# Where VectorE's folds and its small routing steps stand among the top-k scans, in an attention and experts kernel

## The chip, the cores and the metric

The kernel runs on one core of a Trainium2 chip. The metric is the time of one execution on the device, in microseconds, and the figure given for a kernel is the median of several executions. The core has five engines that work at the same time and wait for each other by semaphores: TensorE (matrix products and transposes; PE in the profile, and PEld for its weight loads), VectorE (DVE), ScalarE (ACT), GpSimd (POOL) and SyncE (SP), which issues most of the transfers. Each engine takes its instructions in the order in which they stand in its queue.

## The reference, cut to what matters

Attention keeps, for each query, the keys whose score is among the 32 largest, and its result, rearranged to 4608 rows of 512, goes through a layer of eight experts in which each row is sent to one expert.

```python
# B, H, S, D = 8, 8, 576, 64
scores = scale * np.matmul(q, k.transpose(0, 1, 3, 2))
kth = np.partition(scores, -top_k, axis=-1)[..., -top_k:-top_k + 1]    # top_k = 32
scores = np.where(scores >= kth, scores, -1000000000.0)
attn = np.exp(scores - np.max(scores, axis=-1, keepdims=True))
attn = attn / (np.sum(attn, axis=-1, keepdims=True) + 1e-09)
x = np.matmul(attn, v)                       # then to (B*S, H*D) = (4608, 512)

logits = x @ w_gate                          # 8 experts
expert_idx = np.argmax(logits, axis=1)
probs = np.exp(logits - logits.max(-1, keepdims=True))
probs /= probs.sum(-1, keepdims=True) + 1e-09
gate_w = probs[np.arange(N), expert_idx]
# rows sorted by expert, for each expert e:
h = np.maximum(x_sorted[lo:hi] @ w1[e], 0.0)     # 512 -> 1024
y_sorted[lo:hi] = h @ w2[e]                      # 1024 -> 512
out = gate_w[:, None] * y                        # back in the old order
```

## The kernel before, in words

**Units, groups and iterations.** A unit is two heads of one batch: 8 batches by 4 units. The 576 queries of each head are four tiles of 128 and a rest of 64; the rests of the two heads share one tile. So a unit has nine score tiles of 128 by 576, which are worked on in five groups: four pairs (the same tile of both heads; groups 0 to 3) and a single tile (group 4). One iteration of the main loop (L756) does one group, so there are 160 iterations, 20 for a batch. The order of instructions on TensorE, ScalarE and VectorE is the order of this text (`manual_schedule`, L818); on GpSimd most steps are held to it by `in_turn`.

**One iteration i.** VectorE searches the threshold of group i (`search`, L254). First, `fold` (L246) takes the larger and the smaller of columns k and k + 288 of the scores, so that the scans go over 288 columns and not 576. Then four rounds of `max` (the eight largest, L273) and `match_replace` (strike them out, L282) give the 32 largest of the larger halves, one `max` (L278) the eight largest of the smaller halves, and two small steps (L291 and L295) the threshold `thr`. GpSimd makes `low` of it (L297) and `over` (L300), a sign of whether the search was sure. ScalarE makes of scores and `low` a large number below the threshold and 0 above (Relu, L309), GpSimd subtracts it from the scores (`less`, L318), ScalarE takes the exponential and its row sums `z` (L329), and in the next iteration TensorE transposes the weights (L343, L352) and ScalarE copies them out of PSUM (L346, L355). In the same iteration ScalarE copies the scores of group i + 3 from PSUM (L243), behind the Relu, and TensorE multiplies those of group i + 4 (L234).

**Folds.** The folds of group i + 1 stand in the search of group i, before its last round (`between`, L761). A pair's search folds the next pair; where a single tile follows, it folds that and the pair behind it, and the single tile's search folds nothing.

**Ends of units.** `ending` (L665) is a generator that goes on at named places of the loop (`at_place`, L721): value products (L373), the transposes of the result (L379), `divisors` (L394: `doubt`, the sums with an epsilon, their reciprocals and a copy from the upper half of the partitions to the lower), `logits` and `rows` (L402, L412: GpSimd scales by the reciprocals). Behind the last unit of a batch come `route` (L418) and `table` (L493).

**Routing.** `route` finds each row's expert (`oh` is one where the row's expert is), takes the exponential of the logits, and on TensorE counts the rows before each one with the same expert (L436) and the rows of each tile of 128 (L437). ScalarE copies both to SBUF (`rk`, L440). VectorE sums the tiles' counts up to `base` and to the new `run` (L445), adds them to the ranks, picks the row's own (`posi`), and the divisor of the gate (L459 to L461). Then GpSimd scatters the batch's rows to DRAM (`x_rows`, L466) by five indirect DMAs, one an iteration. `table` works on one partition: which blocks of 128 rows have become full, as a list of expert and place for the next blocks.

**Expert blocks.** A block is 128 rows of one expert, in 16 pieces of TensorE's work. From the third batch on, pieces are spread over the iterations as far as blocks are full: 4, 4, 5, 4, 5 and 4 of them are announced by the tables of batches 1 to 6, and a batch's rate begins at its iteration `FIRST`. In the last batch, from iteration `ARRIVED` on, all but the pieces of two blocks are spread over what is left; those two cover the last routing. The other 14 of 40 blocks come behind the loop. `load_block` (L540) reads the table on SyncE and loads rows and weights, two blocks ahead.

**PSUM.** `bank` (L199) gives one of two banks in turn, for transposes, value products and the rank product alike.

Of the kernel before, what the change touches and what calls it, by code (L numbers as in the profile page):

```python
# [18 lines left out]
TOP_K = 32  # L19
# [24 lines left out]
def kernel(  # L44
# [94 lines left out]
    e_less = iota_f("e_less", [P, E], [[1, E]], base=-E)  # L139
    e_at = iota_f("e_at", [P, E], [[CAP, E]])  # L140
# [18 lines left out]
    doubt = const.tile([P, NT], F32, name="doubt")  # L159
# [7 lines left out]
    nc.vector.memset(done, 0.0)  # L167
# [45 lines left out]
    def open_unit(n):  # L213
        n.z = k.small.tile([P, NT], F32, name="z")
        n.over = None if k.exact else k.small.tile([P, NT], F32, name="over")
# [30 lines left out]
    def fold(tiles, s):  # L246

        m2 = slice(0, len(tiles))
        hl = k.att.tile([P, 2, 2, HF], F32, name="hl") if len(tiles) == 2 else k.att.tile([P, 2, 1, HF], F32, name="hl1", bufs=1)
        nc.vector.tensor_tensor(hl[:, 0, m2, :], s[:, m2, 0, :], s[:, m2, 1, :], op=ALU.max)  # L250
        nc.vector.tensor_tensor(hl[:, 1, m2, :], s[:, m2, 0, :], s[:, m2, 1, :], op=ALU.min)
        return hl

    def search(n, tiles, s, hl, begun, between):  # L254
# [5 lines left out]
        if k.exact:  # L260
            src = [s[:, m, :, :].rearrange("p j k -> p (j k)") for m in m_all]
            width = S
        else:
            src = [hl[:, 0, m, :] for m in m_all]
            width = HF
        scr = k.att.tile([P, 2, width], F32, name="scr")
        nbias = k.small.tile([P, 2], F32, name="nbias", bufs=3)
        R = TOP_K // 8
        for r in range(R):
            if r == R - 1:  # L270
                between()
            for m in m_all:
                nc.vector.max(out=tops[:, m, r * 8:(r + 1) * 8], in_=src[m])  # L273
            if r == 0:
                in_turn(nc.gpsimd.tensor_scalar_mul(nbias[:, m2], tops[:, m2, 0], -scale))
                if not k.exact:
                    for m in m_all:
                        nc.vector.max(out=tops[:, m, TOP_K + 1:TOP_K + 9], in_=hl[:, 1, m, :])  # L278
                begun()
            if r < R - 1:  # L280
                for m in m_all:
# [3 lines left out]
                    )  # L285
                    src[m] = scr[:, m, :]
# [107 lines left out]
    def divisors(n):  # L394
        rz = rz_of[n.u % 2]
        if not k.exact:
            nc.vector.tensor_tensor(doubt, doubt, n.over, op=ALU.max)
        nc.vector.tensor_scalar_add(rz[:, 0:NT], n.z, EPS)
        nc.vector.reciprocal(rz[:, 0:NT], rz[:, 0:NT])
        nc.vector.tensor_copy(rz[0:ST, NT:NT + 1], rz[ST:P, NT - 1:NT])  # L400

# [16 lines left out]
    def route(x, lg):  # L418

        mx = k.small.tile([P, KC], F32, name="mx")  # L420
        nc.vector.tensor_reduce(mx, lg, axis=AX.X, op=ALU.max)
        oh = k.small.tile([P, KC, E], F32, name="oh")
        nc.vector.tensor_tensor(oh, lg, _inner(mx[:, :], E), op=ALU.is_ge)
        nc.vector.tensor_tensor(oh, oh, _ins(e_less[:, :], 1, KC), op=ALU.mult)
        idx = k.small.tile([P, KC], F32, name="idx")
        nc.vector.tensor_reduce(idx, oh, axis=AX.X, op=ALU.min)
        nc.vector.tensor_tensor(oh, _ins(e_less[:, :], 1, KC), _inner(idx[:, :], E), op=ALU.is_equal)
        nc.vector.memset(oh[ST:P, NC, :], 0.0)

        nc.vector.tensor_tensor(lg, lg, _inner(mx[:, :], E), op=ALU.subtract)  # L430
        yield
        nc.scalar.activation(lg, lg, AF.Exp)
        yield
        rp = bank("rank")
        ohf = oh[:, :, :].rearrange("p t e -> p (t e)")
        nc.tensor.matmul(rp[:, 0:KC * E], before, ohf, start=True, stop=True)  # L436
        nc.tensor.matmul(rp[:, 256:256 + KC * E], ones, ohf, start=True, stop=True)  # L437
        yield
        rk = k.small.tile([P, 2, KC * E], F32, name="rk")
        nc.scalar.copy(rk, rp[:, :].rearrange("p (a w) -> p a w", a=2)[:, :, 0:KC * E])  # L440
        yield
# [492 lines left out]
```

## Time and profile before

| | us |
|---|---|
| median of 7 executions | 1630.79 (1627.06 to 1636.61) |
| the profiled execution | 1630.93 |
| its span, first to last instruction | 1628.9 |
| batches 0 to 7: time from one batch's last threshold to the next one's (the first from 10.4) | 150.3, 160.1, 164.7, 168.5, 170.1, 172.4, 168.3, 170.3 |
| last threshold of the loop | 1335.4 |
| VectorE, top-8 scans (L273, L278), 1440 instructions | 592.3 busy |
| VectorE, strike-outs (L282), 864, with their loads of values | 447.0 busy |
| VectorE, folds (L250, L251), 320 | 253.3 busy |
| GpSimd, `less` (L318), 288 | 404.4 busy, 1423 ns each |

The table's busy times are sums of the recorded durations. Records of one engine can overlap: a scan is recorded with 0.45 us, but the next one starts 0.36 us after it. So what an instruction costs its engine is better read from the distance between starts in the timeline. A group's line also names the idle time of the engine before it and what ended it; only on the engine that is full does that time count. TensorE's granted clock differs between the parts: 0.78 between 40 and 160 us, where there are no expert blocks, and 0.93 to 0.95 in batches 3 to 7.

### The profile page before, as it was taken

What the parts mean: (1) busy time and instruction counts of PE and PEld (TensorE: products, weight loads), DVE (VectorE), ACT (ScalarE), POOL (GpSimd) and SP (SyncE); (2) the same over time, 40 slices, a digit from 0 to 9 for tenths busy, and PEclk for the clock granted to TensorE, in tenths of its full rate; (3) what the DMA queues carried; (4) which work ended last, traced back from release to release, by engine and by line L of the source; (5) the groups of instructions that cost most, each with busy time, mean ns of one, the idle gap of its engine ahead of it and who ended that gap; (6) DMA issues with size and microseconds to landing.
All of it is one profiled execution on the core that took longest, in us unless ns stands there. A gap on an engine that the chain in (4) does not pass through costs nothing. (4 is left out here: it accounts for less than half of the span.)

```text
span 1628.9 us, 25051 instructions
## 1 busy us (share of the span) xinstructions
PE 1334.3 (82%) x7874; PEld 868.6 (53%) x7874; DVE 1284.2 (79%) x4261; ACT 917.1 (56%) x1937; POOL 667.1 (41%) x993
## 2 busy tenths in 40 slices
PE   5666766664889889978987998799898998799996
PEld 3333433332555555545654655555565656566764
DVE  7999999999999999999998999999989972000000
ACT  4666656665676576657666766667666762111111
POOL 3444454445445454435444544455455442000000
PEclk8777677777899899989998999899998999899998
DMA  1000010001624244344446433334353545788783
GB/s 60 24 23 23 23 49 26 24 24 49 245 90 146 99 150 141 136 147 149 140 177 230 156 140 139 124 135 167 139 174 140 198 154 190 268 322 292 288 332 129
DMA packets 102192, 230.69 MB, mean 142 GB/s; under 512 B 5150, under 2 KB 25630, under 8 KB 102048
## 3 DMA queue, kind: packets, MB, share of 16 engines
q1 hardware_dynamic: 95904, 210.06, 36.3%
q0 software_dynamic: 6144, 18.92, 3.2%
q8 instruction: 65, 1.06, 0.3%
q14 instruction: 79, 0.65, 0.1%
HBM read 207.68 MB, written 22.33 MB: 141 GB/s over the span
## 5 line engine op out<-in xcount | busy, mean ns | idle before, releaser
L318 POOL TENSOR_TENSOR w<-s,w 128x576 f32<-128x576 f32 x288 | 404.4, 1423 | 287.1 <-ACT w L309 287.1
L273 DVE MAX8 tops<-scr 128x8 f32<-128x288 f32 x864 | 356.8, 451 | 3.3
L575 PEld LDWEIGHTS ph<-xTs,w 128*128 128x128 f32 x2560 | 300.7, 193 | 31.7 <-issue 29.0
L575 PE MATMUL ph<-xTs,w 128*128 128x128 f32 x2560 | 312.2, 278 | 5.7 <-DMA w<-in_moe_w_dram 3.1
L309 ACT ACTIVATE w<-s,low 128x576 f32<-128x576 f32 x288 | 208.9, 769 | 190.3 <-POOL low L297 188.4
L584 PE MATMUL py<-w,hT 128*128 128x512 f32 x640 | 308.5, 614 | 6.3 <-ACT hT L580 6.3
L234 PE MATMUL sc<-qkb 64*128 64x288 f32 (+1 forms) x1280 | 243.9, 506 | 70.2 <-ACT s L243 63.6
L282 DVE MATCH_REPLACE8 scr<-tops,scr 128x288 f32<-128x288 f32 x576 | 251.9, 446 | 0.0
L329 ACT ACTIVATE w<-w,nbias 128x576 f32<-128x576 f32 x288 | 221.6, 772 | 1.8 <-POOL w L318 1.8
L343 PE MATMUL wTm<-ident,w 128*128 128x128 f32 x1152 | 180.1, 295 | 42.9 <-ACT oT L375 33.7
L234 PEld LDWEIGHTS sc<-qkb 64*128 64x128 f32 (+1 forms) x1280 | 123.9, 207 | 143.6 <-ACT s L243 80.7
L343 PEld LDWEIGHTS wTm<-ident,w 128*128 128x128 f32 x1152 | 138.7, 150 | 110.2 <-ACT oT L375 41.0
L297 POOL TENSOR_SCALAR low<-thr 128x2 f32<-128x2 f32 (+1 forms) x160 | 35.0, 219 | 361.3 <-DVE thr L295 342.6
L584 PEld LDWEIGHTS py<-w,hT 128*128 128x128 f32 x640 | 114.2, 194 | 117.5 <-issue 106.1
L243 ACT COPY s<-sc 128x576 f32<-128x576 f32 x288 | 170.1, 638 | 9.9 <-PE sc L234 9.9
L373 PE MATMUL po<-wT,vb 128*64 128x288 f32 x1024 | 172.6, 490 | 0.6 <-ACT wT L348 0.6
L352 PE MATMUL wTl<-ident,w 128*64 128x128 f32 x288 | 65.4, 304 | 125.2 <-ACT wT L346 123.8
L346 ACT COPY wT<-wTm 128x512 f32<-128x512 f32 x256 | 140.1, 606 | 11.2 <-PE wTm L343 11.1
L250 DVE TENSOR_TENSOR hl<-s 128x576 f32<-128x576 f32 (+1 forms) x160 | 129.3, 808 | 12.4 <-ACT s L243 12.4
L590 POOL DMA_INDIRECT out_dram<-y,xg x40 | 41.9, 1048 | 236.1 <-ACT y L587 232.3
L373 PEld LDWEIGHTS po<-wT,vb 128*64 128x64 f32 x1024 | 81.3, 165 | 89.1 <-issue 35.0
L282 DVE MATCH_REPLACE8 scr<-tops,hl 128x288 f32<-128x288 f32 x288 | 125.7, 444 | 0.0
(123 smaller groups left out, 1362.8 us busy)
## 6 DMA issues: line engine op xcount, KB each, us to landing
w<-in_moe_w_dram SPq DMA_DIRECT2D x80, 2048.0 KB, 9.1
qkb<-in_qk_dram SPq DMA_DIRECT2D x32, 576.0 KB, 5.0
xg<-x_rows SPq DMA_DIRECT2D x40, 257.0 KB, 2.7
vb<-in_v_dram SPq DMA_DIRECT2D x32, 320.0 KB, 3.1
x_rows<-blank SPq DMA_DIRECT2D x9, 257.0 KB, 5.4
x_rows<-x,posi POOLq DMA_INDIRECT x40, 3.1
out_dram<-y,xg POOLq DMA_INDIRECT x40, 3.0
wg<-in_moe_w_gate_dram SPq DMA_DIRECT2D x1, 16.0 KB
```

Source lines behind the costliest of these rows:

```text
L234: nc.tensor.matmul(ps[rows, j, 0:HF], n.q[d, cols], n.k[d, j * HF:(j + 1) * HF], start=True, stop=True)
L243: lambda m=m, ps=ps: nc.scalar.copy(s[:, m, :, :], ps[:, :, 0:HF]) for m, ps in enumerate(got)
L273: nc.vector.max(out=tops[:, m, r * 8:(r + 1) * 8], in_=src[m])
L282: nc.vector.match_replace(out=scr[:, m, :], in_to_replace=tops[:, m, r * 8:(r + 1) * 8], in_values=src[m], imm_value=NEG,)
L309: nc.scalar.activation(w[:, m, :], s[:, m, :, :].rearrange("p j k -> p (j k)"), AF.Relu, scale=-STEEP, bias=low[:, m:m + 1],)
L318: k.last_pool = in_turn(nc.gpsimd.tensor_tensor(w[:, m, :], s[:, m, :, :].rearrange("p j k -> p (j k)"), w[:, m, :], op=ALU.subtract)).ins
L329: nc.scalar.activation(w[:, m, :], w[:, m, :], AF.Exp, scale=scale, bias=nbias[:, m:m + 1], accum_out=n.z[:, c + m:c + m + 1],)
L343: nc.tensor.transpose(pm[:, c * P:(c + 1) * P], w[:, m, c * P:(c + 1) * P], ident)
L346: nc.scalar.copy(n.wT[:, :, m, tiles[0] * P:(tiles[0] + 1) * P], pm4)
L373: nc.tensor.matmul(po[r, 0:HF], lhsT, rhs, start=(c == 0), stop=(c == KC - 1))
L575: nc.tensor.matmul(ph[:, f, :], n.w1[:, 0, dt, fc * P:(fc + 1) * P], n.xT[:, dt, :], start=(dt == 0), stop=(dt == DT - 1),)
L584: nc.tensor.matmul(py, hT[:, f, :], n.w2[:, 0, f, :], start=(f == 0), stop=(f == FT - 1))
```

## The change

**Folds.** The folds of group i + 1 stand before the search of group i, that is directly behind the threshold of group i - 1. They write two tiles, `h` and `l`, in place of one.

**Small steps between scans.** `divisors`, the choice of the expert, the positions and the table become generators of single steps. They are put on a list, `aside`; `tick`, called in the search behind a scan or a strike-out (for pairs from the second round on, ten times a search; for single tiles from the third, three times), takes the next one. `through` issues what is left of a generator at the place where its result is needed.

**`doubt`.** `over` is written straight into a tile for all units, so the step that collected it in `divisors` is gone; one reduction over all of it stands behind the loop.

**Routing.** A constant, `e_same`, takes the place of the step that cleared the unused rows of `oh`. The counts of the tiles before and the old `run` are added to the ranks by further products in the same PSUM bank, the new `run` likewise; ScalarE copies only `run`. VectorE reads the positions from PSUM. `table` has 15 steps in place of 21 (for the last one, other numbers).

**Places.** `logits` and `rows` go from the first round of a search (behind `nbias`) to the place behind `less` of the iteration before. The positions are worked out two iterations later than before, the table's steps in the two searches behind; the scatters start three iterations later, and `FIRST` and `ARRIVED` go from 12 to 13.

```diff
+    e_same = const.tile([P, KC, E], F32, name="e_same")
+    nc.vector.tensor_copy(e_same, _ins(e_less[:, :], 1, KC))
+    nc.vector.memset(e_same[ST:P, NC, :], 1.0)
...
-        n.over = None if k.exact else k.small.tile([P, NT], F32, name="over")
+        n.over = None if k.exact else doubt[:, n.b * U + n.u, :]
...
     def fold(tiles, s):
 
         m2 = slice(0, len(tiles))
-        hl = k.att.tile([P, 2, 2, HF], F32, name="hl") if len(tiles) == 2 else k.att.tile([P, 2, 1, HF], F32, name="hl1", bufs=1)
-        nc.vector.tensor_tensor(hl[:, 0, m2, :], s[:, m2, 0, :], s[:, m2, 1, :], op=ALU.max)
-        nc.vector.tensor_tensor(hl[:, 1, m2, :], s[:, m2, 0, :], s[:, m2, 1, :], op=ALU.min)
-        return hl
+        h = k.att.tile([P, 2, HF], F32, name="h")
+        nc.vector.tensor_tensor(h[:, m2, :], s[:, m2, 0, :], s[:, m2, 1, :], op=ALU.max)
+        l = k.att.tile([P, 2, HF], F32, name="l")
+        nc.vector.tensor_tensor(l[:, m2, :], s[:, m2, 0, :], s[:, m2, 1, :], op=ALU.min)
+        return h, l
+
+    aside = []
+
+    def tick():
+
+        while aside:
+            if next(aside[0], "end") != "end":
+                return
+            aside.pop(0)
+
+    def through(steps):
+        for _ in steps:
+            pass
+        if steps in aside:
+            aside.remove(steps)
...
+        def quiet(r):
+
+            return r >= (1 if len(tiles) == 2 else 2)
+
         for r in range(R):
-            if r == R - 1:
-                between()
             for m in m_all:
                 nc.vector.max(out=tops[:, m, r * 8:(r + 1) * 8], in_=src[m])
+                if quiet(r):
+                    tick()
...
                     nc.vector.match_replace(
...
+                    if quiet(r):
+                        tick()
...
     def divisors(n):
         rz = rz_of[n.u % 2]
-        if not k.exact:
-            nc.vector.tensor_tensor(doubt, doubt, n.over, op=ALU.max)
         nc.vector.tensor_scalar_add(rz[:, 0:NT], n.z, EPS)
+        yield
         nc.vector.reciprocal(rz[:, 0:NT], rz[:, 0:NT])
+        yield
         nc.vector.tensor_copy(rz[0:ST, NT:NT + 1], rz[ST:P, NT - 1:NT])
+        yield
...
+    def choice(lg):
...
+        def steps():
+            nc.vector.tensor_reduce(mx, lg, axis=AX.X, op=ALU.max)
+            yield
+            nc.vector.tensor_tensor(oh, lg, _inner(mx[:, :], E), op=ALU.is_ge)
+            yield
+            nc.vector.tensor_tensor(oh, oh, _ins(e_less[:, :], 1, KC), op=ALU.mult)
+            yield
+            nc.vector.tensor_tensor(lg, lg, _inner(mx[:, :], E), op=ALU.subtract)
+            yield
+            nc.vector.tensor_reduce(idx, oh, axis=AX.X, op=ALU.min)
+            yield
+            nc.vector.tensor_tensor(oh, e_same, _inner(idx[:, :], E), op=ALU.is_equal)
+            yield
...
+    def ranks(r):
+
         rp = bank("rank")
-        ohf = oh[:, :, :].rearrange("p t e -> p (t e)")
-        nc.tensor.matmul(rp[:, 0:KC * E], before, ohf, start=True, stop=True)
-        nc.tensor.matmul(rp[:, 256:256 + KC * E], ones, ohf, start=True, stop=True)
...
+        ohf = r.oh[:, :, :].rearrange("p t e -> p (t e)")
+        r.pos, r.run = rp[:, 0:KC * E], rp[:, 256:256 + E]
+        nc.tensor.matmul(r.pos, before, ohf, start=True, stop=False)
+        for i in range(1, KC):
+            nc.tensor.matmul(rp[:, i * E:KC * E], ones, ohf[:, 0:(KC - i) * E], start=False, stop=False)
+        nc.tensor.matmul(r.pos, ident, _ins(run[:, :], 1, KC), start=False, stop=True)
         for i in range(KC):
-            nc.vector.tensor_tensor(
-                base[:, i + 1, :] if i < NC else run[:, :], base[:, i, :],
-                rk[:, 1, i * E:(i + 1) * E], op=ALU.add,
-            )
+            nc.tensor.matmul(r.run, ones, r.oh[:, i, :], start=(i == 0), stop=False)
+        nc.tensor.matmul(r.run, ident, run, start=False, stop=True)
...
+    def places(r, x):
...
+            nc.vector.tensor_tensor(pos, r.pos.rearrange("p (t e) -> p t e", e=E), r.oh, op=ALU.mult)
+            yield
+            nc.vector.tensor_reduce(den, r.lg, axis=AX.X, op=ALU.add)
+            yield
+            nc.vector.tensor_reduce(posf, pos, axis=AX.X, op=ALU.add)
+            yield
+            nc.vector.tensor_scalar_add(den, den, EPS)
+            yield
+            nc.vector.tensor_copy(r.posi, posf)
+            yield
+            nc.vector.reciprocal(x[:, :, Dm], den)
+            yield
...
-    FIRST = 12
-    ARRIVED = 12
+    FIRST = 13
+    ARRIVED = 13
...
             yield "weights"
+            yield "small"
+            div = divisors(n)
+            aside.append(div)
             yield "products"
...
-            yield "small"
-            divisors(n)
-            yield "begun"
+            yield "pool"
+            through(div)
             logits(n, lg)
             rows(n, x)
             if u < U - 1:
                 return
+            yield "weights"
             yield "small"
-            steps = route(x, lg)
-            next(steps)
+            r = choice(lg)
+            aside.append(r.steps)
+            yield "weights"
             yield "turn"
-            next(steps)
+            through(r.steps)
+            nc.scalar.activation(lg, lg, AF.Exp)
             yield "products"
-            next(steps)
+            ranks(r)
             yield "weights"
-            next(steps)
+            nc.scalar.copy(run, r.run)
             yield "small"
-            scatters.extend(next(steps))
+            steps = places(r, x)
+            aside.append(steps)
+            yield "pool"
+            yield "pool"
+            through(steps)
+            scatters.extend(scattering(r, x))
...
+                steps = table(slot_i, new, b == B - 1)
+                aside.append(steps)
+                yield "weights"
+                yield "pool"
+                yield "weights"
+                yield "pool"
+                through(steps)
...
-            fold_to(0)
+            hl_of[0] = fold(work[0][2], s_of[0])
             for i, (b, u, g) in enumerate(work):
...
-                low, nbias = search(n, g, s_of[i], hl_of.pop(i), lambda: at_place("begun"), between)
+                if i + 1 < len(work):
+                    hl_of[i + 1] = fold(work[i + 1][2], s_of[i + 1])
+                low, nbias = search(n, g, s_of[i], *hl_of.pop(i))
                 at_place("small")
...
                 scatter(1)
+                at_place("pool")
                 at_place("relu")
```

## The prediction

> **What bounds the kernel now.** I read the page's busy table and its slices first, then the stretches batch by batch, then VectorE's timeline, then POOL's and ScalarE's beside it. The profiled execution took 1630.93 us (span 1628.9 and 2.0 around it), against a median of 1630.79, so sums made on the profile hold for the median as they stand.
>
> ```profile
> PE 1334.3 (82%) x7874; PEld 868.6 (53%) x7874; DVE 1284.2 (79%) x4261; ACT 917.1 (56%) x1937; POOL 667.1 (41%) x993
> DVE  7999999999999999999998999999989972000000
> ...
> 654.00:824.10 170.10, 147.93 (x913) 96.39 (x912) 163.05 (x533) 109.01 (x235) 81.49 (x120) 0.93 0.39 138
> 1164.80:1335.10 170.30, 153.90 (x973) 102.58 (x972) 161.67 (x532) 113.81 (x242) 83.17 (x122) 0.95 0.46 163
> 1392.60:1628.90 236.30, 215.16 (x1192) 153.14 (x1192) 0.00 (x0) 34.87 (x57) 14.69 (x15) 0.97 0.75 276
> ```
>
> The columns of the stretches are PE, weight load, VectorE, ScalarE and POOL busy, then TensorE's clock, the DMA share and GB/s. VectorE is full from 10 to 1335 us (95 to 96% of the two batches shown), then has nothing; the last 236 us are expert blocks on TensorE. So the scan loop is bound by VectorE, with one reservation: from batch 3 on TensorE is busy 87 to 90%.
>
> VectorE's records overlap, so an instruction's cost is the distance to the next start.
>
> ```profile
> 636.97 0.76 DVE L250 TENSOR_TENSOR hl<-s 128x576 f32<-128x576 f32 x1
> 637.64 0.76 DVE L251 TENSOR_TENSOR hl<-s 128x576 f32<-128x576 f32 x1
> 638.31 0.82 DVE L273 MAX8 tops<-scr 128x8 f32<-128x288 f32 x2
> ...
> 639.53 0.16 DVE L397 TENSOR_TENSOR doubt<-doubt,over 128x9 f32<-128x9 f32 x1
> 639.61 0.17 DVE L398 TENSOR_SCALAR rz<-z 128x9 f32<-128x9 f32 x1
> 639.81 0.21 DVE L399 RECIPROCAL rz<-rz 128x9 f32<-128x9 f32 x1
> 640.06 0.15 DVE L400 COPY rz<-rz 64x1 f32<-64x1 f32 x1
> 640.22 0.46 DVE L273 MAX8 tops<-hl 128x8 f32<-128x288 f32 x1
> ...
> 626.50 3.29 POOL L318 TENSOR_TENSOR w<-s,w 128x576 f32<-128x576 f32 x2 [4.18 <-ACT w L309]
> ...
> 627.20 1.32 DVE L250 TENSOR_TENSOR hl<-s 128x576 f32<-128x576 f32 x1
> 628.44 1.96 DVE L251 TENSOR_TENSOR hl<-s 128x576 f32<-128x576 f32 x1
> 630.33 0.81 DVE L273 MAX8 tops<-scr 128x8 f32<-128x288 f32 x2
> ```
>
> The reader is to see two things. A step with no tie to its neighbour costs 0.08 us (639.53 to 639.61); behind one that it needs, 0.20 to 0.25. And a pair's two folds cost 1.34 us alone but 3.13 when POOL's large subtract (L318) runs beside them. The scans, with one input each, keep their 0.36 us.
>
> **The change part by part, on VectorE.** *Routing and table.* In the old order the second half of the routing is one block between two scans:
>
> ```profile
> 696.36 0.16 DVE L443 COPY base<-run 128x8 f32<-128x8 f32 x1
> 698.72 0.77 DVE L445 TENSOR_TENSOR base<-base,rk 128x8 f32<-128x8 f32 x4 [2.20 <-ACT rk L440]
> ...
> 702.12 0.12 DVE L497 TENSOR_TENSOR lo<-run,e_at 1x8 f32<-1x8 f32 x1
> 706.00 0.80 DVE L273 MAX8 tops<-hl 128x8 f32<-128x288 f32 x2
> ```
>
> That is 9.64 us: 2.4 waiting for ScalarE's rank copy, 3.4 in sums and positions, 3.9 in 21 table steps. From threshold to threshold a pair takes 8.0 us; the first pair of a batch's second unit exceeds that by 4.2 (batch 1, no table), then 9.3, 7.8, 9.5, 7.7, 9.3 and 7.7: 55.5. The seven steps of the first half cost 2.0 by their starts, seven times inside the loop: 14. Together 69.5 us. After the change 6 + 6 + 15 steps remain, nearly all between independent scans, at 0.08 to 0.12 us; I take 0.10. Only three ticks fall into the single tile's search, so three of the first six stand in a row (0.45), and the comparison may meet POOL (0.4, from its mean of 0.61 against 0.20). That is 1.2 + 0.6 + 1.5 = 3.3 a batch, 1.8 without a table: 21.6. Gain 48. If a step between scans still cost 0.20, it would be 27 steps by 0.1, 2.7 a batch less: 29.
>
> *Divisors.* 639.53 to 640.22 is 0.69; three steps between scans cost 0.08, 0.13 and, for the copy across partitions whose 0.16 I keep, some 0.1 of extra wait before it: 0.47. 31 units: 7. The doubt reduction behind the loop grows from 9 to 288 elements, one step, hidden by the closing blocks.
>
> *Folds and thresholds.* The starts give 233 us for the folds; alone they would be 256 by 0.667 and 64 by 0.367, or 194. Six of the 39 are two waits for scores (3.2 each), 33 is POOL. The thresholds' first step (L291) costs 16 more than alone, mostly in the single tile's short search. In the new place, 0.09 after a threshold starts, POOL still has to do two tiny steps, and ScalarE its Relu, before the subtract, which now starts 1.36 us after the threshold at the earliest: just as the folds end. Bounds: all 49 gone, or 25 of it still there (17.5 us of the rows multiply L416 and 13.8 of L318 lie today in what would be the folds' new place). The cover is POOL's idleness there; where the subtract is a whole pair late, it is gone, at 0.7 a fold.
>
> The floor of VectorE is so 48 + 7 + 33 + 16 = 104 us lower.
>
> *What is late next.* `low` (POOL) now arrives behind a running fold and waits, as nbias did for 0.72 in place of 0.21 us; Relu, subtract and Exp are queued behind it, about 0.5 us late each time. More important, a pair's scores are needed one search earlier. ScalarE copies them behind the Relu of three tiles before, and those copies end, after that tile's threshold, at a median of 4.2, 2.8, 5.6, 3.8 and 7.5 us (groups 0 to 4), while the new fold wants them at 8, 8, 7.4, 5.2 and 8.
>
> ```profile
> 620.25 0.40 ACT L375 COPY oT<-po 128x288 f32<-128x288 f32 x1 [4.03 <-PE po L373]
> 620.55 1.19 ACT L243 COPY s<-sc 128x576 f32<-128x576 f32 x2
> ```
>
> This is the tight place: 8.0 us after the single tile's threshold (613.69), held by TensorE's value product. Today's lateness alone would make 19 us of waits; a faster VectorE makes more. In a unit with blocks I follow it through: rows on POOL end 11 us after the third threshold, so the next `low` stays there and the scores behind it at 22.4; the old order then needed 40.7 us a unit, the new one 38.9, with 37.3 as VectorE's floor. Gain 1.8 for 20 units, not 3.4.
>
> *TensorE.* Five batches need 703 us of full clock (busy by clock, 136 + 138 + 147 + 137 + 146), and 12 rank products in place of 2 add 2 us a batch. VectorE's floor for them is 5 by (4 by 37.3 + 3.3) = 762. TensorE would be at 93%; it held 91% busy at clock 0.97 in the blocks alone. The two batches with five blocks (147 + 2, at 0.95) cannot go under 157, and the last loads fall into 7 iterations instead of 8. I add 14. The rank bank is one of two that transposes rotate through and is now held until VectorE reads it, 4 us into a search: a microsecond a batch, within that.
>
> *Queues.* No DMA is added. The five scatters of a batch leave POOL three iterations later, and the block loads on SP follow by one (FIRST 13); with the loads two blocks deep and 140 GB/s moving, nobody waits, except as just counted. *Ends.* The second fold now stands before the first search: scores at 12.55, fold done 10.91, so 1.6 us more. In the tail TensorE waits for the last rows:
>
> ```profile
> 1392.60 1.09 PE L560 MATMUL xtp<-ident,xg 128*128 128x128 f32 x4 [10.47 <-DMA xg<-x_rows]
> ```
>
> so the last routing is on the path: 2.1 us of position sums (1359.71 to 1361.8) and the copy's 0.25 become 0.9 plus 0.6 for more rank products: 1.5 less.
>
> **The sum.** Batches 3 to 7: 20 by 1.8 = 36, routing 5 by 7 = 35, less 14: 57. Batches 0 to 2: routing 12 (4.2 + 9.3 + 2 by 2.0 - 5.1), and 0.5 for each of 12 units, less 1 for waits: 17. Ends: nothing net. 1630.9 - 74 = 1557; since `low`'s half microsecond counts wherever the scores bind, I take 3 off: 1560.
>
> [...]
>
> **Rivals.** *VectorE stays the only bound* and TensorE keeps up: -104 in full, 1527. For it: clock 1.0 wherever PE is dense. Against: in-order queues that both run above 93%. *The shorter look-ahead eats the fold's gain*, routing alone is left: -48 and +1.6, 1585; with steps at 0.2 also 1605. For it: 7.5 against 8 us, and 19 us of waits at today's pace. *Slower:* the same lateness becomes the clock of every unit. The old waits for scores were 3.2 us where they happened; two of them in each of 20 units with blocks are 128, less 104: 1655. It decides from 5.2 us a unit on. Against it: a wait lets ScalarE catch up, so two in one unit need a lateness that renews itself. *Nothing:* TensorE is already the bound from batch 3 and only early batches gain: within 0.3% only if early waits cancel that too.
>
> **How the numbers follow.** Forecast (1540 to 1580) 0.58, full floor 0.10, routing alone 0.17, slower 0.13, nothing 0.02. What this kernel's measurement can tell from no change is 0.3%, 5 us. So faster 0.85, same 0.02, slower 0.13. The range leaves out half of the first rival and the slower one: 1530 to 1605.
>
> **What would show it.** Folds at 0.67 start to start with POOL's subtract behind them; no routing block, pairs at the batch's second unit near 8.5 us; VectorE's idle time ended by ScalarE's score copy at 30 to 60 us in all, in the pairs behind the single tile; TensorE above 90% busy in batches 3 to 7; last threshold near 1265 us. It would be wrong if score waits passed 100 us, or if the loop's end moved and the tail grew by as much.

## The result, and the profile after

| | before | after |
|---|---|---|
| median, us | 1630.42 (77 runs) | 1633.17 (31 runs) |
| lowest to highest | 1624.44 to 1636.61 | 1630.02 to 1639.82 |
| profiled span, us | 1628.9 | 1629.8 |
| first threshold, last threshold, us | 18.8, 1335.4 | 20.3, 1337.5 |

The ratio is 1.002, with a 95% interval of 1.0013 to 1.0027: no gain, within the 0.3% that the prediction took for no change. The forecast was 1560. Below are the page's busy row and VectorE's slices, then the stretch of batches 3 to 7 (from the last threshold of batch 2 to that of batch 7, within 0.4 us) with the columns explained above, all of the kernel after.

```profile
PE 1343.0 (82%) x8034; PEld 890.0 (55%) x8034; DVE 1261.6 (77%) x4130; ACT 918.4 (56%) x1937; POOL 751.8 (46%) x993
DVE  7999999999999989998998989998989881000000
...
472.80:1337.20 864.40, 754.54 (x4792) 509.68 (x4792) 801.16 (x2573) 562.02 (x1195) 462.47 (x608) 0.95 0.41 148
```

The same five batches in the kernel before:

```profile
485.50:1335.10 849.60, 748.16 (x4665) 489.92 (x4665) 813.00 (x2663) 560.48 (x1194) 414.24 (x606) 0.94 0.42 150
```

VectorE has less to do (801 in place of 813 us, and fewer instructions) and the stretch is 14.8 us longer. The slices, nearly all 9 before up to the end of the loop, now have an 8 in many places of the loop's second half. Batches 0 to 2, which have no blocks beside them or few, ended at 473.1 in place of 485.9. So the change does what it was to do while VectorE is alone, and the gain is lost in the batches where TensorE has expert blocks throughout.

The waits say for what. Engine, line, what it waited for, total us, times, longest; the kernel before:

```profile
PE xtp L560 <- DMA xg<-x_rows: 29.5, 14, 10.5
DVE hl L250 <- ACT s L243: 12.4, 3, 5.9
```

and the kernel after:

```profile
PE xtp L620 <- DMA xg<-x_rows: 51.5, 11, 13.7
DVE h L260 <- ACT s L253: 51.4, 13, 6.8
```

VectorE waits 39 us more for scores, and TensorE 22 us more for the rows of expert blocks; inside the loop alone (up to the last threshold) the latter went from 12.1 to 34.2. VectorE's starts between the first and the last threshold put both sides together. Here, and wherever a cost is given "by the starts", a step costs the distance to the next start, and idle time of more than 0.15 us before that start counts as a wait: work 1301.4 before and 1270.8 after, waits 15.2 and 46.5. The 31 us saved were given back in waits, to the microsecond.

One such wait, followed through three engines in the timeline of the kernel after (start, busy us, engine, operation; the wait in brackets):

```profile
579.20 0.96 POOL L517 DMA_INDIRECT x_rows<-x,posi  x1
582.05 0.36 SPq L605 DMA_DIRECT2D xg<-x_rows  x1
584.75 1.11 PE L620 MATMUL xtp<-ident,xg 128*128 128x128 f32 x4 [6.01 <-DMA xg<-x_rows]
585.66 4.64 PE L644 MATMUL py<-w,hT 128*128 128x512 f32 x6
590.45 1.24 PE L244 MATMUL sc<-qkb 64*128 64x288 f32 x8
595.54 1.19 ACT L253 COPY s<-sc 128x576 f32<-128x576 f32 x2
596.76 1.71 DVE L260 TENSOR_TENSOR h<-s 128x576 f32<-128x576 f32 x1 [6.73 <-ACT s L253]
```

It is to be read downwards. The last scatter of a batch leaves POOL, the load of a block's rows is issued behind it, and TensorE is at that moment already at the transposes of that block: it stands for 6.0 us. The products of the next scores (590.45) stand in its queue behind them. ScalarE can copy the scores only at 595.54, and VectorE, which is done with its search, waits 6.7 us for the fold. Six more waits of VectorE stand behind such stand-stills; they end at 767.7, 944.0, 952.8, 1115.5, 1291.3 and 1300.1. In the kernel before, the corresponding load was issued at 577.21 and the transposes came 6.6 us behind it:

```profile
574.33 0.96 POOL L466 DMA_INDIRECT x_rows<-x,posi  x1 [0.16 <-issue]
577.21 0.35 SPq L545 DMA_DIRECT2D xg<-x_rows  x1
583.80 0.42 PEld L560 LDWEIGHTS xtp<-ident,xg 128*128 128x128 f32 x4 [0.39 <-issue]
583.81 0.66 PE L560 MATMUL xtp<-ident,xg 128*128 128x128 f32 x4
```

The small steps don't cost what was taken either. VectorE and POOL behind a threshold at 653 us, in the timeline of the kernel after:

```profile
653.16 0.75 DVE L260 TENSOR_TENSOR h<-s 128x576 f32<-128x576 f32 x1
653.33 0.67 POOL L329 TENSOR_SCALAR low<-thr 128x2 f32<-128x2 f32 x1 [3.54 <-DVE thr L327]
653.83 0.75 DVE L262 TENSOR_TENSOR l<-s 128x576 f32<-128x576 f32 x1
...
654.89 2.79 POOL L350 TENSOR_TENSOR w<-s,w 128x576 f32<-128x576 f32 x2 [0.26 <-ACT w L341]
...
656.79 0.46 DVE L302 MAX8 tops<-scr 128x8 f32<-128x288 f32 x1
657.16 0.55 DVE L428 TENSOR_SCALAR rz<-z 128x9 f32<-128x9 f32 x1
657.62 0.45 DVE L302 MAX8 tops<-scr 128x8 f32<-128x288 f32 x1
657.99 0.19 DVE L430 RECIPROCAL rz<-rz 128x9 f32<-128x9 f32 x1
658.10 0.03 DVE L312 MATCH_VALUE_LOAD scr<-tops,scr 128x8 f32 x1
```

The folds are where the forecast had them, 0.67 apart, done before the subtract (L350) begins. But the first divisor step (L428), 0.46 from its start to the next, now stands under that subtract, and the second, after it ended at 657.68, takes 0.11. Over all its 32 places L428 took a median of 0.46 where it ran beside the subtract (23 times) and 0.07 where it didn't (9).

### The profile page after: what moved, and what is told of

Same layout as the page of the kernel before. It is cut to its first block, busy times and chain, and to the rows that moved or that the text cites. A ratio compares the mean times of both kernels' runs of the same rounds, so it can differ in the third digit from the quotient of the medians.

```text
span 1629.8 us, 25226 instructions
## 1 busy us (share of the span) xinstructions
PE 1343.0 (82%) x8034; PEld 890.0 (55%) x8034; DVE 1261.6 (77%) x4130; ACT 918.4 (56%) x1937; POOL 751.8 (46%) x993
## 3 DMA queue, kind: packets, MB, share of 16 engines
q8 instruction: 66, 1.08, 0.3%
## 5 line engine op out<-in xcount | busy, mean ns | idle before, releaser
L350 POOL TENSOR_TENSOR w<-s,w 128x576 f32<-128x576 f32 x288 | 400.8, 1411 | 237.3 <-ACT w L341 237.3
L302 DVE MAX8 tops<-scr 128x8 f32<-128x288 f32 x864 | 362.2, 450 | 3.1
L635 PE MATMUL ph<-xTs,w 128*128 128x128 f32 x2560 | 323.6, 281 | 2.3 <-ACT xTs L622 2.3
L635 PEld LDWEIGHTS ph<-xTs,w 128*128 128x128 f32 x2560 | 306.0, 195 | 33.5 <-issue 30.8
L244 PE MATMUL sc<-qkb 64*128 64x288 f32 (+1 forms) x1280 | 236.3, 492 | 31.9 <-ACT s L253 25.7
L329 POOL TENSOR_SCALAR low<-thr 128x2 f32<-128x2 f32 (+1 forms) x160 | 81.1, 507 | 353.9 <-DVE thr L327 340.0
L644 PEld LDWEIGHTS py<-w,hT 128*128 128x128 f32 x640 | 118.7, 199 | 126.4 <-issue 113.3
L260 DVE TENSOR_TENSOR h<-s 128x576 f32<-128x576 f32 (+1 forms) x160 | 137.2, 858 | 51.4 <-ACT s L253 51.4
L244 PEld LDWEIGHTS sc<-qkb 64*128 64x128 f32 (+1 forms) x1280 | 122.2, 204 | 100.2 <-ACT s L253 34.9
L405 PE MATMUL po<-wT,vb 128*64 128x288 f32 x1024 | 157.7, 456 | 0.6 <-ACT wT L380 0.6
L312 DVE MATCH_REPLACE8 scr<-tops,h 128x288 f32<-128x288 f32 x288 | 125.6, 444 | 0.0
L405 PEld LDWEIGHTS po<-wT,vb 128*64 128x64 f32 x1024 | 75.5, 152 | 79.5 <-issue 31.2
## 6 DMA issues: line engine op xcount, KB each, us to landing
w<-in_moe_w_dram SPq DMA_DIRECT2D x80, 2048.0 KB, 11.3
```

What stands on the lines that cost most here:

```text
L244: nc.tensor.matmul(ps[rows, j, 0:HF], n.q[d, cols], n.k[d, j * HF:(j + 1) * HF], start=True, stop=True)
L312: nc.vector.match_replace(out=scr[:, m, :], in_to_replace=tops[:, m, r * 8:(r + 1) * 8], in_values=src[m], imm_value=NEG,)
L350: k.last_pool = in_turn(nc.gpsimd.tensor_tensor(w[:, m, :], s[:, m, :, :].rearrange("p j k -> p (j k)"), w[:, m, :], op=ALU.subtract)).ins
L405: nc.tensor.matmul(po[r, 0:HF], lhsT, rhs, start=(c == 0), stop=(c == KC - 1))
L635: nc.tensor.matmul(ph[:, f, :], n.w1[:, 0, dt, fc * P:(fc + 1) * P], n.xT[:, dt, :], start=(dt == 0), stop=(dt == DT - 1),)
L644: nc.tensor.matmul(py, hT[:, f, :], n.w2[:, 0, f, :], start=(f == 0), stop=(f == FT - 1))
```

## The experiments

Four explanations stood. **A, the rows are late:** the five scatters of a batch leave three iterations later, the load only one iteration later in TensorE's queue, and TensorE stands. **B, the folds come too early:** they want a pair's scores one search sooner, so any lateness becomes a wait (the rivals' look-ahead). **C, TensorE is the bound** from batch 3 on, so that nothing on VectorE matters there. And, beside these, **the small steps** between scans cost more than in a row. "Before" was measured beside each group of runs on the same chip (medians 1630.4 to 1631.7); ratios are to it, with 95% intervals. What is said to lie "in the loop" ends before the last threshold; the lists of waits are of the whole execution.

| kernel | median, us | ratio |
|---|---|---|
| e1, after, three scatters an iteration | 1605.63 | 0.9857 (0.9833 to 0.9881) |
| e2, after, folds back before the last round | 1654.56 | 1.0156 (1.0131 to 1.0181) |
| e3, before, with the folds moved alone | 1637.38 | 1.0040 (1.0026 to 1.0053) |
| e4, after, no step between scans | 1628.31 | 0.9991 (0.9974 to 1.0008) |
| e5, e1 with the folds back | 1627.97 | 0.9988 (0.9975 to 1.0002) |
| e6, e1, only the table's steps between scans | 1593.24 | 0.9783 (0.9760 to 0.9807) |
| e7, e6, fold behind the first scan | 1598.52 | 0.9804 (0.9777 to 0.9831) |
| e8, before, rows and table three iterations later | 1677.28 | 1.0293 (1.0269 to 1.0317) |
| g1, e6, all five scatters at once | 1603.57 | 0.9829 (0.9810 to 0.9848) |
| g2, e6, scores four iterations ahead | 1600.30 | 0.9807 (0.9790 to 0.9825) |
| g3, e6 with the folds back | 1607.55 | 0.9852 (0.9824 to 0.9880) |
| g4, after, scores four iterations ahead | 1627.81 | 0.9977 (0.9963 to 0.9992) |

**e1: the rows sooner.** In the loop, ahead of the step of POOL's first place:

```diff
-                scatter(1)
+                scatter(3)
```

> The changed kernel with three scatters an iteration in place of one, so that a batch's rows are complete, and the next block's load issued, about two iterations earlier, where they were before the change. Theory A (late rows: TensorE stands at the transpose of a block's rows that have not landed, and everything behind it is late): TensorE's wait for the rows falls from 52 to under 20 us, VectorE's wait for scores from 51 to under 20, and the time to 1595 to 1610. Theory B (the folds' new place: scores are wanted a search earlier, and POOL's steps are held up by the folds): the waits move elsewhere, the time stays above 1620. Theory C (TensorE is the bound in batches 3 to 7): no more than 5 us.

It is 27.5 us faster than the kernel after. Its waits:

```profile
DVE h L260 <- ACT s L253: 25.8, 9, 5.1
PE xtp L620 <- DMA xg<-x_rows: 25.3, 8, 12.0
```

Both halved, to 25 us and not to the under 20 that A had expected; in the loop TensorE's wait for rows fell from 34.2 to 9.2 us, less than in the kernel before (12.1), and VectorE's for scores from 44.5 to 19.1. VectorE's work by the starts stayed (1270.5), and the last threshold came at 1311.6, 26 us sooner. So the whole gain is in waits, and the time is the one that A had forecast, with folds and small steps as they were.

**e8: the rows later, in the kernel before.** The same delay without the rest of the change:

```diff
-            scatters.extend(next(steps))
+            puts = next(steps)
+            for _ in range(3):
+                yield "relu"
+            scatters.extend(puts)
...
-    FIRST = 12
-    ARRIVED = 12
+    FIRST = 13
+    ARRIVED = 13
```

> The kernel before with nothing changed but that the five scatters of a batch (and its table) leave three iterations later and FIRST and ARRIVED are 13, as in the changed kernel. Theory A: TensorE's wait for rows rises from 30 to about 50 us, score waits of VectorE to 20 or more, the time to 1645 to 1660. If late rows matter only together with the folds' new place: within 5 us of before.

It is 47 us slower than the kernel before, more than was expected:

```profile
PE xtp L560 <- DMA xg<-x_rows: 63.8, 21, 14.4
DVE hl L250 <- ACT s L243: 38.5, 8, 6.9
```

26 us of it are score waits (38.5 for 12.4), as A has it. Another 19 is VectorE's own: by the starts the table rose from 23.2 to 36.0 and the routing from 38.5 to 44.8, because the table, delayed with the rows, now stands beside POOL's subtract: 12 of its 126 steps took over 0.4 us each, all while the subtract ran, and none of them met it in the kernel before. So e8 shows that the delay by itself makes the waits, and its size is not a clean measure of them.

**g1: all five rows at once**, on e6, `scatter(5)` in place of `scatter(3)`.

> As the run with rows early and ticks for the table alone (1593), with all five scatters of a batch in one iteration. Theory A, carried further: TensorE's wait for rows falls from 28 to about 15 us and the time to 1583 to 1591. Against it: five scatters in a row hold POOL 5.5 us, low behind them is late once a batch; then 1593 within 5.

It is 10 us slower than e6. TensorE's wait for rows stayed (28.6 against 27.7 us), VectorE's for scores rose from 22.2 to 36.7. Some 11 us behind the first of the five scatters a wait for scores now ends in each of the seven batches inside the loop: five new ones of 1.4 to 2.0 us, and two that grew from 2.6 to 5.2 and 5.9, 13.4 of the 14.5 us together. A scatter holds POOL for 1.03 us in e6, five in a row thus for some 5 us, and ScalarE's longest wait for `low` between 400 and 1300 us is 6.1 us in place of 3.6: five in a row hold up `low` and all that follows. Three an iteration is the better end of A.

**e2, e5, g3: the folds back** before the last round of a search, as they stood in the kernel before: on after, on e1, on e6.

```diff
+                def between():
+                    if len(g) == 2:
+                        for j in range(i + 1, i + 2 if i + 1 < len(work) and len(work[i + 1][2]) == 2 else i + 3):
+                            if j < len(work):
+                                hl_of[j] = fold(work[j][2], s_of[j])
...
-                if i + 1 < len(work):
-                    hl_of[i + 1] = fold(work[i + 1][2], s_of[i + 1])
-                low, nbias = search(n, g, s_of[i], *hl_of.pop(i))
+                low, nbias = search(n, g, s_of[i], *hl_of.pop(i), between)
```

> The changed kernel with the folds back at their old place, before the last round of the scans; all else as changed, the late rows too. Theory B: score waits of VectorE nearly vanish (under 10 us of the 51) and the time falls to 1600 to 1615. Theory A: TensorE still waits about 50 us for rows, the time stays within 8 us of the changed kernel's. Theory C: within 5 us of it.

> The changed kernel with the rows early (three scatters an iteration) and the folds back before the last round of scans. If the folds' new place is worth something by itself: slower than the 1606 of rows early alone, 1615 to 1635, with more collisions of folds and the GpSimd scaling of rows. If the shorter look-ahead were what holds the changed kernel back (theory B): faster, 1580 to 1600, with no score waits.

> As the run with rows early and ticks for the table alone (1593), with the folds back before the last round of scans. If the new place is worth something by itself: 1605 to 1620, with more time in folds and in the single tile's threshold. If in the earlier run with the folds back it was only the ticked steps that waited (for row sums and the run count): 1593 within 5.

Each is slower than its base: by 21, 22 and 14 us. If the early folds were the cause, putting them back had to gain. In e2, TensorE's wait for rows stays at 53.0 and VectorE's for scores at 44.5, and two more come up in the loop, 14.2 us at the positions (2.0 in the kernel after) and 5.5 at the divisors (none); that is against B, and it is also a miss for A, which had the folds' place as nearly neutral. In e5 the score waits do fall, to 12.9, but 25 us in the loop stand at the divisors and the positions in their place (1.8 in e1; the profiled execution of e5 lies 8 us under its median, so these show the kind of wait rather than the exact size). The further collisions of folds that were expected of e5 hardly came: 219.5 us of folds by the starts, 217.7 in e1. What g3 says, where both other parts are mended, is the cleanest: the folds' new place is worth 14 us there. By the starts the folds cost 242.2 us in g3 and 222.6 in e6.

**e3: the folds moved alone**, in the kernel before.

```diff
+                fold_to(i + 1)
-                low, nbias = search(n, g, s_of[i], hl_of.pop(i), lambda: at_place("begun"), between)
+                low, nbias = search(n, g, s_of[i], hl_of.pop(i), lambda: at_place("begun"), lambda: None)
```

> The kernel before with only the folds moved behind the threshold. Theory B: 10 to 30 us slower than before, with 30 us or more of score waits and POOL's low at 0.5 us and more in place of 0.22. Theory A: not slower, and up to 20 us faster, since the collisions of folds and subtract become fewer. Theory C: within 5 us.

It is 7 us slower than before. None of A, B and C had that. Score waits rose from 12.4 to 20.5 us, the folds went by the starts from 224.2 only to 218.3 while the searches rose by 2.7, and `low` took 464 ns in place of 218. The move by itself is thus no gain: with the old routing the waits that it brings outweigh the collisions that it takes away. The same move gains 14 us in g3's pair, where rows and routing are out of the way.

**e7: does `low` behind a running fold cost anything?** On e6, the fold stands behind the first scan of the search, so that `low` can run ahead of it. In the kernel after, `low` took a median of 0.66 us beside a fold (126 times) and 0.22 clear of one (34). If this lateness mattered, e7 was to be 5 to 15 us faster than e6; if not, within 4 us of it, or a little slower where the second fold meets the subtract.

```diff
+                if r == 0 and m == 0:
+                    between()
...
+                def between():
+                    if i + 1 < len(work):
+                        hl_of[i + 1] = fold(work[i + 1][2], s_of[i + 1])
```

> As the run before, with the next group's fold behind the first scan of a search instead of directly behind the threshold. [...]

`low` is back near its old size; e6 and e7:

```profile
L329 POOL TENSOR_SCALAR low<-thr 128x2 f32<-128x2 f32 x128 | 56.4, 441 | 326.7 <-DVE thr L327 207.6 <-DVE rz L428 116.0 <-PE wTm L375 3.2
L331 POOL TENSOR_SCALAR low<-thr 128x2 f32<-128x2 f32 x128 | 30.5, 238 | 327.5 <-DVE thr L329 208.3 <-DVE rz L430 118.4 <-PE wTm L377 0.7
```

(out<-in, shapes, count | busy, mean ns of one | idle before, by what.) That is 238 ns, against 441 in e6 (521 in the kernel after), and the kernel is no faster than e6 (5 us slower by the medians; the intervals overlap). Taking away the lateness that the prediction named first gained nothing that could be measured.

**e4: no step between scans.** On after, `quiet`, which decides whether a step may be laid behind a scan, returns `False`, so that every step stands in a row at its due place.

> The changed kernel without ticks: the small steps stand in a row where their result is asked for, behind a threshold. If a step between scans saves the 0.1 us that the prediction took for each, some 27 steps a batch and 3 a unit, the time is 20 to 28 us longer than the changed kernel's. If the steps between scans meet POOL's subtract and so cost about 0.2 us each, as in a row, it is within 6 us of it.

It is some 5 us faster than after by the medians. By the starts the divisors cost 19.4 us in place of 21.8, choice and places 12.7 in place of 22.9, and the table 28.4 in place of 17.7. So laying steps between scans gains for the table and loses for all the rest. In a row, 12 of the table's 90 steps took over 0.4 us beside POOL's subtract, 14.7 us in all, and the others 0.18 each; between scans it is 14 steps, 11.3 us and 0.08. Choice and places, in a row, stood clear of the subtract, at 0.15 us a step.

**e6: only the table between scans**, on e1. This combines what e1 and e4 said:

```diff
-            aside.append(div)
...
-            aside.append(r.steps)
...
-            aside.append(steps)
```

(the last one is that of the places; the table's stays.)

> Rows early, and ticks for the table alone: divisors, choice and places stand in a row where their results are asked for. If the 128-partition steps lose by standing beside POOL's subtract (divisors 21.8 against 19.4 us, choice and places 22.9 against 12.7 in the runs with and without ticks) and the one-partition table gains (17.7 against 28.4): 8 to 14 us faster than rows early alone, 1592 to 1598. If the ticks make no difference at all: 1606 within 4.

It is 12.4 us faster than e1 and 37 faster than before: the best of all, as expected. By the starts the divisors cost 19.4 us, choice 8.3, places 5.2, table 12.5. L428 in the group list of the kernel after,

```profile
L428 DVE TENSOR_SCALAR rz<-z 128x9 f32<-128x9 f32 x32 | 16.1, 503 | 7.0 <-ACT w L361 7.0
```

and of e6:

```profile
L428 DVE TENSOR_SCALAR rz<-z 128x9 f32<-128x9 f32 x32 | 5.2, 164 | 7.0 <-ACT w L361 7.0
```

A step of 164 ns takes 503 ns on average when it is put where POOL is at work. The five last batches of e6,

```profile
473.50:1297.60 824.10, 747.11 (x4792) 503.71 (x4792) 789.78 (x2573) 561.86 (x1194) 452.06 (x608) 0.96 0.43 155
```

take 40 us less than in the kernel after with the same 4792 matmuls. TensorE was busy for 91% here and 87% there: it was not the bound, and C is out.

**g2 and g4: one more iteration of look-ahead.** If the early folds' shorter look-ahead were the limit, computing scores four iterations ahead in place of three had to help, on e6 (g2) and on after (g4).

```diff
-    AHEAD = 3
+    AHEAD = 4
...
-        s = k.att.tile([P, 2, 2, HF], F32, name="s", bufs=2 if k.exact else 4)
+        s = k.att.tile([P, 2, 2, HF], F32, name="s", bufs=2 if k.exact else 5)
...
-        scr = k.att.tile([P, 2, width], F32, name="scr")
+        scr = k.att.tile([P, 2, width], F32, name="scr", bufs=1)
...
-        y = k.mlp.tile([P, Dm], F32, name="y")
+        y = k.mlp.tile([P, Dm], F32, name="y", bufs=1)
```

(The last two make room for the fifth score buffer.)

> As the run with rows early and ticks for the table alone (1593), with scores computed four groups ahead instead of three (a fifth score buffer; one buffer less for the scans' scratch and for the blocks' result). Theory B (the folds' new place shortens the look-ahead and VectorE waits for scores): its waits fall from 22 to under 6 us and the time to 1575 to 1586. Theory C (TensorE sets the pace by then): within 4 us.

> The changed kernel, late rows and all ticks, with scores four groups ahead. If late rows cost time only by way of late scores, one group more of look-ahead covers most of it: 1600 to 1615. If TensorE's stand-still itself is what is lost: above 1622.

g2 has almost no score waits left (6.8 us in two), and is no faster than e6 (7 us slower by the medians; the intervals just overlap), which neither B nor C had. Part of what took their place is in the step that joins the two halves' best values; e6,

```profile
L323 DVE TENSOR_TENSOR both<-tops 128x18 f32<-128x18 f32 x128 | 31.9, 249 | 4.2
L323 DVE TENSOR_TENSOR both<-tops 128x9 f32<-128x9 f32 x32 | 9.7, 302 | 1.1
```

and g2:

```profile
L323 DVE TENSOR_TENSOR both<-tops 128x18 f32<-128x18 f32 x128 | 40.3, 315 | 4.2
L323 DVE TENSOR_TENSOR both<-tops 128x9 f32<-128x9 f32 x32 | 15.2, 474 | 1.1
```

VectorE, no longer waiting, reaches it more often while POOL still subtracts (53 of the 159 in the loop, 36 in e6), and by the starts the step costs 14 us more. g4 is 5 us faster than the kernel after, though its score waits fell from 51.4 to 8.5:

```profile
PE xtp L620 <- DMA xg<-x_rows: 54.9, 15, 13.2
DVE rz L428 <- ACT w L361: 34.9, 9, 7.0
```

TensorE stands for the rows as before, and VectorE now waits for ScalarE's row sums at the divisors (27.9 us of the 34.9 in the loop, where the kernel after has none). ScalarE's queue in turn holds copies of what TensorE makes late: at 593.43 it had waited 6.29 us for a block's transposes. So look-ahead is not the limit: with the rows late, one group more of it only moved the waits to another step. With one buffer less in two places, both kernels may also carry a cost; it was not measured by itself.

## Why the prediction was wrong, step by step

**What bounds the kernel: right.** VectorE for batches 0 to 2, and VectorE with a busy TensorE after; e6 shows that the loop could still give 37 us with no less work for TensorE.

**Queues: this is the step that failed.** It said that the scatters leave POOL three iterations later, the block loads follow by one, and "nobody waits, except as just counted". It saw both numbers and did not set them against each other. Between last scatter and transposes the kernel before had 9.5 us (574.33 to 583.81); a delay of the rows by three iterations against one for the block eats that and more, and TensorE's queue holds the score products behind the transposes. What the runs showed in its place: TensorE stood 34.2 us for rows in the loop, not 12.1, and VectorE waited 44.5 us for scores; with the rows early again it was 9.2 and 19.1. Price: 27.5 us, the distance of after to e1; e8 shows the waits arising in the kernel before from the same delay.

**Small steps at 0.10 us: wrong.** Price 12.4 us in e6 against e1. Routing and table were put at 69.5 before, and were 70.3 by the starts (38.5, 8.6 of waits, 23.2); after the change they cost 42.6 (11.7, 11.2, 2.0 of waits, 17.7) in place of the 21.6 that were taken. The gain was 28, not 48: about the 29 of the case in which a step still costs 0.20. In e6 they cost 26.0, and this term came nearly whole. The divisors gained nothing (21.3 to 21.8) in place of 7. The error is that 0.08 was read from untied steps at 639.5, while POOL did only two tiny steps (0.21 and 0.19 us); the new places lie behind the folds, where POOL subtracts. The prediction knew that POOL's subtract makes a fold slow, and allowed 0.4 for one comparison a batch; it did not apply it to steps with one input.

**Folds and thresholds: the bounds were too hopeful.** All 49 us of collisions gone was one end, 25 of them still there the other; the folds went from 224.2 to 220.3 us only, the thresholds' first step from 58.5 to 50.1: 12 us in place of 24 to 49. The fold's 0.67 is there where the subtract comes behind it, as at 653 us; but 28 of the pairs' h folds still take some 1.63 us beside it, 27 us too much in all, and among them are all 11 that had waited for scores. And small steps now stand beside the subtract: L428 alone costs about 9 us more for it (23 places at 0.46 in place of 0.07). In e6 the two terms are back at 222.6 and 57.2, a gain of 3. The new place is worth 14 us in g3 against e6, because there the old place costs more than it did in the kernel before (242.2 us of folds).

**What is late next: size right by luck, cause wrong.** Waits for scores of 30 to 60 us were foreseen, and 51.4 came. But they were to come from the shorter look-ahead, and from `low` half a microsecond late each time. e7 takes `low`'s lateness away and gains nothing; most of the waits come in lumps of 2 to 7 us behind TensorE's stand-still, and half of them leave with the rows in e1. The look-ahead has a share: the move of the folds alone raised the score waits by 8 us in e3. The slower rival named the right symptom, waits for scores, but it needed 5.2 us of them a unit; 44.5 us in 20 units are 2.2. And neither of the prediction's two signs of being wrong came, score waits over 100 us or a longer tail.

**TensorE: right that it does not bind, wrong on its share.** Above 90% busy in batches 3 to 7 was said; it was 87%, with 34.2 us of waits for rows, and e6 reaches 91%.

**Early batches and ends: right.** Batches 0 to 2 ended 12.7 us sooner, 14 without the start (17 forecast); the start is 1.5 later (1.6), the tail 1.2 shorter (1.5).

**The sum.** Forecast minus 74, measured plus 3. Of the 73 us that are missing against 1560, late rows are 27.5 and the small steps 12.4, and e6 stands at 1593. No run separates the other 33, but the starts in e6 point to where most of them lie. Against the kernel before, routing and table gained 44 of the 48 us (70.3 to 26.0), the divisors 2 of 7, and folds and thresholds 3, where the floor had 49; score waits in the loop rose by 9 (6.5 to 15.6). So even in the best kernel the folds are the term that did not come: 222.6 us against 194 undisturbed. Whether they can be taken down was not tried.

**The order of the steps.** It matters here, in both directions: 0.07 us free and 0.46 beside POOL for the same step. The mean of a step between scans was 0.20 us in the table (0.32 in a row), 0.23 in the divisors (0.21) and 0.27 in choice and places (0.15).

## What to carry to other kernels

When a change delays what a transfer reads, put the new issue time against the place of the transfer's consumer in its in-order queue, and ask what stands in that queue behind the consumer: here 6 us in front of a transpose cost VectorE nearly 7 us, through scores that had nothing to do with it. A cheap step is only cheap at its new place: before small steps are laid between others, look at what the other engines do there (the same step, L428, took 0.46 us beside POOL's subtract and 0.07 clear of it). And measure parts of a change apart: of a change that gave nothing as a whole, the late rows cost 27 us and the badly placed steps 12, while the folds' new place gained 14 beside the other two mended, and the best kernel kept what gained (1593.24 us, 0.9783 of the time before).

## What the runs showed of the hardware

Here TensorE's stand-still cost more than its length. The stretches around 584 us in the kernel after, with TensorE's clock third from the end:

```profile
575.00:584.70 9.70, 2.07 (x17) 1.64 (x15) 9.56 (x32) 3.84 (x7) 5.72 (x8) 0.89 0.37 100
584.70:590.40 5.70, 5.65 (x12) 2.82 (x12) 5.20 (x21) 0.59 (x1) 0.00 (x0) 0.58 0.98 379
590.40:596.00 5.60, 5.60 (x32) 3.59 (x31) 0.00 (x0) 4.45 (x11) 0.93 (x1) 1.00 0.90 333
```

After 6 us without a product the granted clock was 0.58 for the next 5.7 us, though TensorE was busy for 5.65 of them, and six products py that took 2.82 us at 593 took 4.64 at 585.66: 1.8 us more, in front of the same scores. In the 5.6 us behind that it was 1.00. So the clock of 1.0 wherever PE is dense, which the prediction's first rival counted on, did not hold right behind this stand-still.

Not every small step of VectorE took longer beside POOL's subtract. In the kernel after, choice and places, laid between scans:

```profile
L502 DVE TENSOR_SCALAR den<-den 128x5 f32<-128x5 f32 x8 | 7.0, 880 | 0.0
L504 DVE CAST posi<-posf 128x5 int32<-128x5 f32 x8 | 3.1, 383 | 0.1
L467 DVE TENSOR_REDUCE idx<-oh 128x5 f32<-128x40 f32 x8 | 1.5, 190 | 0.0
L500 DVE TENSOR_REDUCE posf<-pos 128x5 f32<-128x40 f32 x8 | 1.5, 190 | 0.0
```

In e6, where they stand in a row:

```profile
L502 DVE TENSOR_SCALAR den<-den 128x5 f32<-128x5 f32 x8 | 1.3, 162 | 0.0
L504 DVE CAST posi<-posf 128x5 int32<-128x5 f32 x8 | 1.4, 172 | 0.6
L467 DVE TENSOR_REDUCE idx<-oh 128x5 f32<-128x40 f32 x8 | 1.5, 193 | 0.0
L500 DVE TENSOR_REDUCE posf<-pos 128x5 f32<-128x40 f32 x8 | 1.6, 197 | 0.0
```

By the means, an addition of a constant to 5 elements (L502) grows fivefold and a conversion (L504) doubles; the reductions don't change. In the kernel after, L502 took a median of 0.81 us in the 7 of its 8 places beside the subtract and 0.16 in the other, L504 1.08 in 2 beside it and 0.15 in 6 clear of it. The reduction L500 stood beside it in 7 places and took 0.19 there as in the eighth (0.20); L467 never met it. The scans too (L302) kept their distance to the next start, a median of 0.37 us in 426 beside the subtract and in 726 clear of it. And a longer POOL record is not yet a loss: e7 takes `low` from 441 ns to 238 and is no faster.
